# Placing K and Q on the diagonal by ScalarE, head by head, in a chunked delta-rule attention kernel

## The chip, the cores and the metric

The kernel runs on one core of a Trainium2 chip. The metric is the device time of one launch in microseconds (us). The kernel before was timed in three runs; a change of time is judged against their median.

## The reference

Three stages follow one another. Only the first, a gated delta rule over 4 batches, 8 heads, 768 positions and head size 48, is touched by the change:

```python
k_n = k / (norm(k) + 1e-6)
state = zeros((B, H, 48, 48))
for t in range(768):
    y[:, :, t] = q[t] @ state                     # per batch and head
    v_old = state.T @ k_n[t]
    state = state + beta[t] * outer(k_n[t], v[t] - v_old)
```

The second stage is a mixture of 8 experts with one expert per token (3072 tokens, 384 wide, 1024 hidden). The third is a gated feed-forward layer with 1536 hidden. All in float32.

## The kernel before, in words

The attention works in 24 steps of 32 positions. A step handles all 4 batches and 8 heads at once: two of the four batches share the 128 partitions (head dimension of one on rows 0 to 47, of the other on rows 64 to 111), and a second index p = 0, 1 tells the two such pairs apart. To multiply both batches of a pair in one matmul, the stationary operand is block diagonal: of its 64 columns, columns 0 to 31 hold the positions of the first batch and are zero on the lower rows, columns 32 to 63 hold those of the second and are zero on the upper rows. These operands are the tiles KB (12 of them, used in a ring, `RK`) and QB (two, in turn). Their layout is [128, p, 64 positions, 8 heads], so the 64 columns of one head lie 8 elements (32 bytes) apart.

A step s goes through these matmul groups on TensorE (PE), each of 16 products (8 heads, p = 0 and 1) unless noted; a float32 product shows as two instructions, so a group of 16 is listed as x32:

- KS: KB against the state SH; VectorE (DVE) then makes W from it (L802, L803).
- Y, first part: QB against the state (L818, and L859 for the six last products in steps from 19).
- U: TBD, the inverted triangle, against W (L827). ScalarE (ACT) and DVE split the result into UH, high and low.
- XTP: three transposes for the gate of the step before (`gate_t`).
- GP: KB of step s + 11 against KT, the raw K and Q of that step (`gp_mm`, L219), in two pieces, 24 instructions here and 8 later, for steps 1 to 12. The moving operand KT also has its columns 8 elements apart.
- Sps: the state's update in float16; ACT copies it to SH for the next step (L876).
- Y, second part, in float16, then GL, the gate's logits (12 instructions, stationary columns side by side).

DVE also computes, four steps at a time, the inverse of a 32 x 32 triangle for each of the 32 chunks (tiles X, Lt, XT). These many small operations are put between the others by a planner (`Filler`) with a fixed budget of modelled time for each step (`TA`, `TB`, `TP`); each engine executes its own instructions in the order written. The inverse of group 0 goes into TBD partly by copies, partly by a transfer on the queue of SyncE (SP) (`expand_rest`, L402).

Transfers of the attention are issued on SP's queue in the order written. In step s: KT of step s + 12 (`load_kt`), the diagonal of QB for step s + 1 (`fill`, two transfers), after KS the diagonal of KB for step s + 12 (`fill`, two transfers, for s up to 11), expansions of P and of normalized K (PBD, KBD), loads of K and V by token, and for s up to 4 `zero_fill` of one expert's first 512 rows in the dispatch table in HBM. `zero_fill` takes its zeros from half of TBD[1] and sends one row of 386 elements 16 times from each of 32 partitions. Before step 0, diagonals for steps 0 to 11 and three zero fills are issued in the same way. POOL (GpSimd) zeroes the off-diagonal blocks once, before the loop, and scatters finished rows to the dispatch table from step 6 on.

Of the kernel before, what the change touches and what calls it, by code (L numbers as in the profile page):

```python
# [7 lines left out]
F32 = mybir.dt.float32  # L8
# [13 lines left out]
NSTEP, NG = SEQ // CH, SEQ // CH // 4  # L22
# [3 lines left out]
STRIDE = 3136 + WIN  # L26
WINS = (460, 436, 416, 404, 396, 388, 380)
WMAX = 460
XMAX = 512
ROW = 386  # L30
# [4 lines left out]
LA = 11  # L35
# [35 lines left out]
RK = LA + 1  # L71
# [70 lines left out]
class Attention:  # L142
# [5 lines left out]
    def run(self, small, acc, zero_fill, small_loads):  # L148
        tc, a, beside = self.tc, self.a, self.beside
        nc = tc.nc  # L150
        V, A, G = [Queue(tc, e) for e in (nc.vector, nc.scalar, nc.gpsimd)]
        T, SP = Queue(tc, nc.tensor), Queue(tc, nc.sync)
        engines = (V, A, G, T, SP)
        ctx, early = ExitStack(), ExitStack()
        wk = ctx.enter_context(tc.tile_pool(name="at_w", bufs=1, side="right"))
# [13 lines left out]
        zf = cp.tile([128, 128], F16, name="zf")  # L169
        zl = cp.tile([128, 128], F16, name="zl")  # L170
        KB = [(ep if i < 8 else cp).tile([128, 2, 64, 8], F32, name=f"KB{i}") for i in range(RK)]
        QB = [cp.tile([128, 2, 64, 8], F32, name=f"QB{i}") for i in range(2)]
        TBD = [(cp if i else ep).tile([128, 32, 2, 32], F32, name=f"TBD{i}") for i in range(2)]
        PBD = [cp.tile([128, 2, 16, 4, 32], F16, name=f"PBD{i}") for i in range(2)]
        KBD = [cp.tile([128, 2, 2, 8, 2, 64], F16, name=f"KBD{i}") for i in range(2)]
# [9 lines left out]
        def fill(dst, s, k, rows=48):  # L185
            for par in range(2):
                r = slice(64 * par, 64 * par + rows)
                ins = SP.dma_start(
                    out=dst[r, :, 32 * par : 32 * par + 32].rearrange("p a t h -> p a (t h)"),
                    in_=a["st"][s, r].rearrange("p (k a x) -> p k a x", k=2, a=2)[:, k])  # L190
            return ins.ins

        def load_kth(u):
            t = wk.tile([128, 2, 48, 8], F32, tag="kth", name="kth", bufs=1)
            SP.dma_start(out=t.rearrange("p s d h -> p s (d h)"), in_=a["ktok"][:, 2 * u : 2 * u + 2])
            KTOK[u] = t

        def load_v(u):
            t = wk.tile([128, 2, 384], F32, tag="VT", name="VT", bufs=2)
            SP.dma_start(out=t, in_=a["vtok"][:, 2 * u : 2 * u + 2])  # L200
            VT[u] = t
# [10 lines left out]
        def gp_mm(s, hs, mm=T.matmul):  # L212
            if s not in GPS:
                tag = {4: "KS", 5: "Y", 7: "XTP", 8: "GL", 9: "U"}.get(s, "GP")
                GPS[s] = pool(tag).tile([128, 8, 64], F32, tag=tag, name="GP", bufs=1)
            ps, t = GPS[s], KT[s]
            for h in hs:
                for p in range(2):
                    mm(out=ps[64 * p : 64 * p + 64, h], lhsT=KB[s % RK][0:112, p, :, h], rhs=t[0:112, :, p, :, h], start=True, stop=True)  # L219

        G0 = {}

# [42 lines left out]
        def gp_evac(s):  # L265

            ps = GPS.pop(s)
            KT.pop(s)
            g, s4 = divmod(s, 4)
            if s4 == 0 and g > 0:  # L270
                GPM[g] = [ep.tile([128, 32, 32], F32, tag=n, name=n, bufs=b) for n, b in (("G", 2), ("P", 2))]
            A.copy(out=GPM[g][0][:, 8 * s4 : 8 * s4 + 8], in_=ps[:, :, 0:32])
            return A.copy(out=GPM[g][1][:, 8 * s4 : 8 * s4 + 8], in_=ps[:, :, 32:64]).ins
# [49 lines left out]
        def kexp(u):  # L323
            KH = KHG.pop(u)
            for b in range(4):
                SP.dma_start(
                    out=KBD[u % 2][32 * b : 32 * b + 32, :, :, :, b % 2, 0:48].rearrange("p s a h d -> p (s a h) d"),
                    in_=KH[32 * b : 32 * b + 32].rearrange("p s a h d -> p (s a h) d"))
# [56 lines left out]
                fil.step()  # L385

        XTS, others = {}, []
        zeros = TBD[1].rearrange("p k b i -> p (k b i)").rearrange("p (b x) -> p b x", b=2)

        def share_rows(n):  # L390
            for f in others[:n]:
# [231 lines left out]
        def zap_off(E, t):  # L623

            for par in range(2):
                r = t[64 * par : 64 * par + 64, :, 32 - 32 * par : 64 - 32 * par].rearrange("p a t h -> p a (t h)")
                E.memzero(r) if E is A else E.memset(r, 0.0)
# [46 lines left out]
        zap_off(G, KB[7])  # L674
        zap_off(A, KB[5])
        zap(A, PBD[0], 2)
        zap_off(G, QB[0])
        zap_off(G, QB[1])
        zap_off(G, KB[8])
        zap(G, PBD[1], 2)  # L680
        for i in range(9, RK):
# [74 lines left out]
        fil.run(99.0)  # L756
        load_kt(LA)
        fill(KB[LA], LA, 0, 64)
        fill(QB[1], 1, 1, 64)
        kexp(1)  # L760
        load_kth(2)
        zero_fill(SP, 2, zeros)
# [15 lines left out]
        for s in range(NSTEP):  # L778
# [8 lines left out]
            if s + 1 + LA < NSTEP:  # L787
                load_kt(s + 1 + LA)
            if 0 < s < NSTEP - 1:
                fill(QB[(s + 1) % 2], s + 1, 1, 64 if s == 1 else 48)  # L790
            beside(s, "load", engines)
            if s > 0:
                W = wk.tile([128, 8, 48], F32, tag="W", name="W", bufs=1)
# [4 lines left out]
            if s > 0:  # L798
                KSf = pp.tile([128, 512], F32, tag="KS", name="KS")
                KSp = KSf[:, 0:384].rearrange("p (h e) -> p h e", h=8)  # L800
                for h, p, r in hp:
                    mm(out=KSp[r, h], lhsT=KB[s % RK][:, p, :, h], rhs=S0[:, p, 48 * h : 48 * h + 48], start=True, stop=True)  # L802
                V.scalar_tensor_tensor(out=W, in0=vp, scalar=SIG * KSC, in1=KSp, op0=ALU.mult, op1=ALU.subtract)  # L803
            beside(s, "W", engines)
            if last:
                flush(gate_v1(g, 0, 2))
            if s + 1 + LA < NSTEP:
                fill(KB[s % RK], s + 1 + LA, 0)
            if s2 == 0 and 0 < s < NSTEP - 2:
                expand(PBD[(u + 1) % 2], PHL.pop(u + 1))  # L810
                if half:
# [3 lines left out]
            ny = NY if s >= LS else 16  # L815
            if s > 0:
                for h, p, r in hp[:ny]:
                    mm(out=Yp[r, h], lhsT=QB[s % 2][:, p, :, h], rhs=S0[:, p, 48 * h : 48 * h + 48], start=(h == 0), stop=False)  # L818
            beside(s, "Y", engines, Sps[0])

            Uf = pp.tile([128, 512], F32, tag="U", name="U", bufs=1)
# [11 lines left out]
            V.tensor_tensor(out=UH[:, 1], in0=Up, in1=UH[:, 0], op=ALU.subtract)  # L833
            if s4 == 0 and g in XE:
                expand_rest(g)
                fil.limit = g + 1
            if s2 == 0:
                if 0 < s < NSTEP - 2:
                    kh_split_lo(u + 1, V)
# [10 lines left out]
            if s == 0:  # L850
                gp_mm(LA, H8, mm)
                gp_evac(LA)
                zero2, other2, ops2 = inv_ops(2, SHE[2])
                fil.add(sum(prep(2), []) + [later(ops2)], 0.5)
            elif more:
                gp_mm(s + LA, H8[:GS], mm)
            else:
                for h, p, r in hp[ny:]:
                    mm(out=Yp[r, h], lhsT=QB[s % 2][:, p, :, h], rhs=S0[:, p, 48 * h : 48 * h + 48], start=(h == 0), stop=False)  # L859
            if last:  # L860
                gate_r(g, mm, 0, 2)
                ops = gate_v2(g, 0, 2)
# [46 lines left out]
            if more and s:  # L909
                gp_mm(s + LA, H8[GS:], mm)  # L910
                gp_evac(s + LA)
            if s == 0:
                expand(PBD[1], PHL.pop(1))
                kh_mul(2, 0)
                p_split(2)
                v_mul(2)
            elif half and s4 != 3:
                kh_mul(u + 2, s2)
                if s2:
                    kh_split_hi(u + 2)  # L920
            if s2 == 1 and half:
                load_v(u + 2)
            if s < 5:
                zero_fill(SP, s + 3, zeros)
            if s == 0:
                zero2()
            elif (s + LA) % 4 == 3 and (s + LA) // 4 < NG:
# [7 lines left out]
                kh_split_hi(u + 2)  # L935
            if s2 == 0 and 0 < s < NSTEP - 2:
                kexp(u + 1)
            beside(s, "end", engines)
            fil.run(((TB - (TP if s2 == 1 and u + 3 < NSTEP // 2 else 0.0) if s + 1 + LA < NSTEP else TC)) if s else TB0)
            if s4 == 3 and half and s < KL:  # L940
# [223 lines left out]
def kernel_body(tc, a, out):  # L1164
    nc = tc.nc
    V, A, G, T, SP = nc.vector, nc.scalar, nc.gpsimd, nc.tensor, nc.sync
    with ExitStack() as ctx:
# [10 lines left out]
        if True:  # L1178
# [6 lines left out]
                SP.dma_start(out=wgo, in_=a["wgo"])  # L1185

            def zero_fill(SP, e, z):
                r = XMAX // 32
                SP.dma_start(out=disp[e * STRIDE : e * STRIDE + 32 * r].rearrange("(p r) c -> p r c", r=r), in_=z[0:32, 1:2, 0:ROW].to_broadcast([32, r, ROW]))

            moe, late_pools = ExitStack(), ExitStack()
            gp = moe.enter_context(tc.tile_pool(name="gt_p", bufs=1, space=PSUM))
# [356 lines left out]
```

## Time and profile before

| what | value |
|---|---|
| median of 3 runs | 1077.36 us (1072.9 to 1080.02) |
| the profiled execution | 1079.89 us, span 1078.2 us |
| PE busy | 1021.3 us, 95% |
| DVE busy | 548.0 us, 51% |
| ACT busy | 397.2 us, 37% |
| POOL busy | 316.9 us, 29% |
| attention | about 0 to 349 us; step 1 begins at 69.05 |

The page of the profile shows for each engine its busy time as a share of the span, and the span in 40 slices. [...] In the slices the clock is at or near half for most of the attention and at full for nearly all that follows.

```profile
PE   9779999998889999899889999999999999999997
DVE  6968988989534577667683374511211211211111
ACT  7534544454453454445444422311212222212111
PEclk9875555665595999999999999999999999999999
DMA  7999988754584364556544122000000000000000
```

### The profile page before, as it was taken

What the parts mean: (1) busy time and instruction counts of PE and PEld (TensorE: products, weight loads), DVE (VectorE), ACT (ScalarE), POOL (GpSimd) and SP (SyncE); (2) the same over time, 40 slices, a digit from 0 to 9 for tenths busy, and PEclk for the clock granted to TensorE, in tenths of its full rate; (3) what the DMA queues carried; (4) which work ended last, traced back from release to release, by engine and by line L of the source; (5) the groups of instructions that cost most, each with busy time, mean ns of one, the idle gap of its engine ahead of it and who ended that gap; (6) DMA issues with size and microseconds to landing.
All of it is one profiled execution on the core that took longest, in us unless ns stands there. A gap on an engine that the chain in (4) does not pass through costs nothing. (4 is left out here: it accounts for less than half of the span.)

```text
span 1078.2 us, 22515 instructions
## 1 busy us (share of the span) xinstructions
PE 1021.3 (95%) x9111; PEld 923.9 (86%) x9112; DVE 548.0 (51%) x1498; ACT 397.2 (37%) x880; POOL 316.9 (29%) x304
## 2 busy tenths in 40 slices
PE   9779999998889999899889999999999999999997
PEld 8679888887889988789889988888888888888886
DVE  6968988989534577667683374511211211211111
ACT  7534544454453454445444422311212222212111
POOL 8530002202012234445444234322321311321322
PEclk9875555665595999999999999999999999999999
DMA  7999988754584364556544122000000000000000
GB/s 193 201 172 204 187 176 154 158 89 102 94 184 121 117 205 153 156 153 183 161 121 128 26 89 74 22 22 1 17 13 1 30 1 1 30 1 1 30 1 30
DMA packets 181438, 102.47 MB, mean 95 GB/s; under 512 B 126841, under 2 KB 170818, under 8 KB 181330
## 3 DMA queue, kind: packets, MB, share of 16 engines
q1 hardware_dynamic: 178258, 91.53, 36.8%
q0 software_dynamic: 3072, 9.46, 2.5%
q8 instruction: 73, 1.20, 0.5%
q14 instruction: 35, 0.29, 0.1%
HBM read 74.94 MB, written 15.80 MB: 84 GB/s over the span
## 5 line engine op out<-in xcount | busy, mean ns | idle before, releaser
L1470 DVE TENSOR_TENSOR gf<-gf,g 128x512 f32<-128x512 f32 x72 | 49.5, 687 | 310.1 <-PE g L1462 310.1
L971 POOL TENSOR_TENSOR gsl<-gf,gsh 128x512 fp32r<-128x512 f32 x68 | 88.4, 1300 | 272.4 <-ACT gsh L970 272.4
L1469 ACT ACTIVATE gf<-g 128x512 f32<-128x512 f32 x72 | 43.0, 597 | 188.5 <-PE g L1462 187.4
L970 ACT CAST gsh<-gf 128x512 fp32r<-128x512 f32 x69 | 42.8, 620 | 144.2 <-DVE gf L1470 142.5
L1436 PE MATMUL o<-woh,gsl 128*128 128x384 f32 x272 | 87.2, 339 | 0.0
L1436 PE MATMUL o<-wol,gsh 128*128 128x384 f32 x272 | 86.5, 337 | 0.0
L87 DVE TENSOR_TENSOR X<-X,tmp 128x84 f32<-128x84 f32 (+37 forms) x303 | 75.0, 277 | 0.8
L87 DVE TENSOR_TENSOR tmp<-X,Lt 128x84 f32<-128x84 f32 (+37 forms) x303 | 72.8, 271 | 1.4
L1151 DVE SCALAR_TENSOR_TENSOR hl<-h,hh 128x460 fp32r<-128x460 f32 (+7 forms) x57 | 33.0, 580 | 64.3 <-ACT hh L1150 64.2
L1110 PE MATMUL y<-hh,w2h 128*128 128x460 f32 (+6 forms) x168 | 60.9, 362 | 2.3 <-ACT hh L1150 2.1
L1462 PE MATMUL g<-yl,wgh 128*128 128x512 f32 x216 | 62.6, 395 | 0.0
L87 PE MATMUL U<-W,TBD 64*64 64x48 f32 x768 | 42.4, 283 | 21.2 <-DVE W L87 13.3
L1462 PE MATMUL g<-yl,wvh 128*128 128x512 f32 x216 | 62.3, 395 | 0.0
L1436 PE MATMUL o<-woh,gsh 128*128 128x384 f32 x272 | 61.7, 337 | 0.0
L87 POOL COPY XG<-g_sc 128x2 f32<-128x2 f32 x24 | 6.0, 248 | 187.5 <-DVE g_sc L87 145.4
L1462 PE MATMUL g<-yh,wgh 128*128 128x512 f32 x180 | 60.9, 395 | 0.0
L87 PEld LDWEIGHTS U<-W,TBD 64*64 64x64 f32 x768 | 38.6, 198 | 24.1 <-DVE W L87 14.9
L1110 PE MATMUL y<-hh,w2l 128*128 128x460 f32 (+6 forms) x168 | 58.6, 349 | 0.0
L87 ACT ACTIVATE ks<-kth,rnt 128x48 f32<-128x48 f32 x192 | 54.5, 371 | 6.9 <-DMA kth<-in_ktok_dram 6.8
L87 PE MATMUL GP<-KT,KB 112*64 112x64 f32 x640 | 47.9, 316 | 9.0 <-DMA KB<-in_st_dram 9.0
L1436 PEld LDWEIGHTS o<-woh,gsh 128*128 128x128 f32 x272 | 49.7, 188 | 5.8
L87 PEld LDWEIGHTS GP<-KT,KB 112*64 112x64 f32 x640 | 42.7, 221 | 13.7 <-POOL KH L87 8.3
(335 smaller groups left out, 2420.1 us busy)
## 6 DMA issues: line engine op xcount, KB each, us to landing
w1r<-in_w_dram SPq DMA_DIRECT2D x32, 384.0 KB
w2r<-in_w_dram SPq DMA_DIRECT2D x32, 384.0 KB
KT<-in_st_dram SPq DMA_DIRECT2D x20, 448.0 KB
disp<-TBD SPq DMA_DIRECT2D x8, 772.0 KB
kth<-in_ktok_dram SPq DMA_DIRECT2D x12, 384.0 KB
VT<-in_vtok_dram SPq DMA_DIRECT2D x12, 384.0 KB
KBD<-KH SPq DMA_DIRECT2D x48, 96.0 KB
XG<-in_m2g_dram SPq DMA_DIRECT2D x12, 384.0 KB
```

The costliest lines, as they stand in the source:

```text
L87: r = f(*args, **kw)
L970: (act or nc.scalar).copy(out=hi, in_=src)
L971: eng.tensor_tensor(out=lo, in0=src, in1=hi, op=ALU.subtract)
L1110: self.T.matmul(out=ys[c][:, 0:n], lhsT=w2[l][:, f % 2, 128 * c : 128 * c + 128], rhs=(hh, hl)[r], start=(f == 0 and i == 0), stop=(f == 7 ...
L1151: self.V.scalar_tensor_tensor(out=hl, in0=hp[:, 0:n], scalar=0.0, in1=hh, op0=ALU.max, op1=ALU.subtract)
L1436: T.matmul(out=ops_[m][:, 0:384], lhsT=gh[l][:, 128 * m : 128 * m + 128], rhs=wo[r][:, f], start=(f == 0 and i == 0), stop=(f == 11 and i ...
L1462: T.matmul(out=ps, lhsT=gv[w][l][:, c, 128 * f : 128 * f + 128], rhs=Y[r][c], start=(i == 0 and c == 0), stop=(i == 2 and c == 2))
L1469: A.activation(out=gf, in_=gps[0], func=AF.Sigmoid)
L1470: V.tensor_tensor(out=gf, in0=gf, in1=gps[1], op=ALU.mult)
```

## The change

QB and the KB tiles that are used a second time (steps 12 to 23) get the layout [128, p, 8 heads, 64 positions], so the columns of one head lie side by side (`kcol`, `by_col`). They are no longer filled by transfers. Two copies on ACT (`place`) take rows 0 to 63 and rows 64 to 111 of raw data that lie in SBUF and write them into the diagonal blocks. For K the raw data is KT, which is loaded anyway; for Q it is a new tile QR with one buffer, loaded by one transfer of 112 rows (`load_q`). `place` for Q of step s + 1 and K of step s + 12 stands at the end of step s, behind the copies of GP from PSUM. POOL zeroes a whole KB tile in each of the steps 0 to 11, since the new layout has its zeros elsewhere. K of steps 0 to 11 keeps the old layout and its transfers. `zero_fill` sends four rows in one run of 1544 elements from each of 128 partitions; its zeros now lie in parts of TBD[1] that group 1's inverse needs first, so experts 3 to 7 are zeroed in steps 0 to 2 in place of steps 0 to 4, and the planner may finish group 1 only from the end of step 2 on (`fil.limit`).

```diff
-        QB = [cp.tile([128, 2, 64, 8], F32, name=f"QB{i}") for i in range(2)]
+        QB = [cp.tile([128, 2, 8, 64], F32, name=f"QB{i}") for i in range(2)]
...
+        by_col = lambda t: t.rearrange("q p t h -> q (p t h)").rearrange("q (p h t) -> q p h t", p=2, h=8)
+        def kcol(s, p, h):
+            return KB[s % RK][:, p, :, h] if s < RK else by_col(KB[s % RK])[:, p, h]
+        def place(dst, src):
+            for par, n in ((0, 64), (1, 48)):
+                r = slice(64 * par, 64 * par + n)
+                A.copy(out=dst[r, :, :, 32 * par : 32 * par + 32], in_=src[r].rearrange("q p t h -> q p h t"))
+        def load_q(s):
+            t = wk.tile([128, 2, 32, 8], F32, tag="QR", name="QR", bufs=1)
+            SP.dma_start(out=t[0:112].rearrange("q p t h -> q (p t h)"), in_=a["st"][s, 0:112, 512:1024])
+            QR[s] = t
...
-                    mm(out=ps[64 * p : 64 * p + 64, h], lhsT=KB[s % RK][0:112, p, :, h], rhs=t[0:112, :, p, :, h], start=True, stop=True)
+                    mm(out=ps[64 * p : 64 * p + 64, h], lhsT=kcol(s, p, h)[0:112], rhs=t[0:112, :, p, :, h], start=True, stop=True)
...
-        fill(QB[1], 1, 1, 64)
+        load_q(1)
...
             if 0 < s < NSTEP - 1:
-                fill(QB[(s + 1) % 2], s + 1, 1, 64 if s == 1 else 48)
+                load_q(s + 1)
...
-                    mm(out=KSp[r, h], lhsT=KB[s % RK][:, p, :, h], rhs=S0[:, p, 48 * h : 48 * h + 48], start=True, stop=True)
+                    mm(out=KSp[r, h], lhsT=kcol(s, p, h), rhs=S0[:, p, 48 * h : 48 * h + 48], start=True, stop=True)
...
             if s + 1 + LA < NSTEP:
-                fill(KB[s % RK], s + 1 + LA, 0)
+                zap(G, KB[s % RK])
...
-                    mm(out=Yp[r, h], lhsT=QB[s % 2][:, p, :, h], rhs=S0[:, p, 48 * h : 48 * h + 48], start=(h == 0), stop=False)
+                    mm(out=Yp[r, h], lhsT=QB[s % 2][:, p, h], rhs=S0[:, p, 48 * h : 48 * h + 48], start=(h == 0), stop=False)
...
-                fil.limit = g + 1
+                fil.limit = g + 1 if g else 0
...
             if more and s:
                 gp_mm(s + LA, H8[GS:], mm)
                 gp_evac(s + LA)
+            if s + 1 < NSTEP:
+                place(QB[(s + 1) % 2], QR.pop(s + 1))
+            if s + 1 + LA < NSTEP:
+                place(by_col(KB[s % RK]), KT[s + 1 + LA][:, 0])
...
-            if s < 5:
-                zero_fill(SP, s + 3, zeros)
+            if s < 3:
+                for e in ((3, 4), (5, 6), (7,))[s]:
+                    zero_fill(SP, e, zeros)
...
+            if s == 2:
+                fil.limit = 1
...
             def zero_fill(SP, e, z):
-                r = XMAX // 32
-                SP.dma_start(out=disp[e * STRIDE : e * STRIDE + 32 * r].rearrange("(p r) c -> p r c", r=r), in_=z[0:32, 1:2, 0:ROW].to_broadcast([32, r, ROW]))
+                SP.dma_start(out=disp[e * STRIDE : e * STRIDE + XMAX].rearrange("(p r) c -> p (r c)", r=XMAX // 128), in_=z[:, 0 : XMAX // 128 * ROW])
```

## Rows read from the trace of the kernel before

**Rows 1.** Busy time by stretch of late steps: stretch, PE, PEld, DVE, ACT, POOL, clock, DMA.

```profile
296.00:322.00 26.00, 22.92 (x534) 21.52 (x531) 9.40 (x25) 13.52 (x35) 3.28 (x5) 1.00 0.85 185
322.00:350.00 28.00, 28.00 (x471) 25.52 (x469) 12.41 (x48) 9.05 (x22) 5.71 (x10) 0.51 0.49 122
```

**Rows 2.** The same view of step 2 and step 3, each from KS to KS.

```profile
87.23:100.59 13.36, 12.60 (x220) 11.77 (x219) 13.26 (x49) 6.15 (x17) 0.00 (x0) 0.50 1.07 208
100.59:113.10 12.51, 12.51 (x220) 11.75 (x219) 10.91 (x39) 6.63 (x18) 0.00 (x0) 0.50 0.91 190
```

**Rows 3.** What PE waited for, 20 to 345 us: total us, times, longest us.

```profile
PE U L87 <- DVE W L87: 13.3, 9, 3.8
PE GP L87 <- DMA KB<-in_st_dram: 9.0, 2, 8.2
PE U L87 <- DMA TBD<-XT: 7.8, 4, 3.8
```

**Rows 4.** Timeline of PE in step 7, clock 0.5: start, duration, instructions, count.

```profile
154.20 2.10 PE L87 MATMUL KS<-SH,KB 128*64 128x48 f32 x32
156.09 2.14 PE L87 MATMUL Y<-SH,QB 128*64 128x48 f32 x32
...
165.53 0.83 PE L87 MATMUL GL<-wgo,xt 128*64 128x16 f32 x12
166.19 0.72 PE L87 MATMUL GP<-KT,KB 112*64 112x64 f32 x8
```

**Rows 5.** Timeline of PE at clock 1.0, steps 12 and 19.

```profile
224.59 1.76 PE L87 MATMUL GP<-KT,KB 112*64 112x64 f32 x24
...
299.63 2.11 PE L87 MATMUL KS<-SH,KB 128*64 128x48 f32 x32
301.56 1.38 PE L87 MATMUL Y<-SH,QB 128*64 128x48 f32 x20
302.87 1.13 PE L87 MATMUL U<-W,TBD 64*64 64x48 f32 x32
303.94 0.55 PE L87 MATMUL XTP<-cst,XG 128*128 128x128 f32 x3
```

**Rows 6.** Timeline of SP's queue before and in step 0, transfers of KB.

```profile
49.48 1.32 SPq L87 DMA_DIRECT2D KB<-in_st_dram  x2
...
67.79 3.35 SPq L87 DMA_DIRECT2D KB<-in_st_dram  x2
```

**Rows 7.** Timeline of PE around the two longest waits for transfers.

```profile
55.41 2.25 PE L87 MATMUL GP<-KT,KB 112*64 112x64 f32 x32 [8.15 <-DMA KB<-in_st_dram]
...
78.71 1.91 PE L87 MATMUL U<-W,TBD 64*64 64x48 f32 x30 [1.36 <-DMA TBD<-XT]
```

**Rows 8.** DMA rate in 40 slices of 30.0 to 34.3, a zero fill alone.

```profile
GB/s 205 158 244 206 186 201 230 244 244 249 263 172 259 230 244 230 215 201 215 187 244 230 215 201 129 215 201 201 215 187 187 172 201 215 187 230 172 115 206 29
```

**Rows 9.** The same of 68.4 to 72.0, a load's end and a zero fill.

```profile
GB/s 325 427 394 377 326 463 360 412 343 377 360 309 309 309 292 223 206 274 223 206 223 240 189 189 223 245 137 223 223 137 206 223 120 223 189 148 302 643 188 410
```

**Rows 10.** Timeline of ACT in step 7.

```profile
154.71 0.38 ACT L87 COPY P<-GP 128x256 f32<-128x256 f32 x1
155.11 2.29 ACT L87 ACTIVATE ks<-kth,rnt 128x48 f32<-128x48 f32 x8
160.16 0.48 ACT L87 CAST UH<-U 128x384 f16<-128x384 f32 x1 [2.76 <-PE U L87]
```

**Rows 11.** Instructions by tile, ACT and POOL: count, shortest/median/longest ns, first and last start.

```profile
L87 ACT CAST PHL<-P x10: 601/610/622, 81.0 to 291.3; 128x512 f16<-128x512 f32 x10
L87 ACT CAST KH<-ks x24: 494/504/512, 31.0 to 310.1; 128x384 f16<-128x384 f32 x24
L87 ACT ACTIVATE ks<-kth,rnt x192: 361/370/395, 26.6 to 309.5; 128x48 f32<-128x48 f32 x192
L1040 ACT ACTIVATE XR<-XR x24: 600/602/620, 391.5 to 570.1; 109x384 f32<-109x384 f32 x4, 104x384 f32<-104x384 f32 x4, 101x384 f32<-101x384 f32 x4, 99x384 f32<-99x384 f32 x4
L87 POOL MEMSET QB<- x4: 518/520/523, 9.9 to 11.6; 64x512 f32 x4
```

More of the change, by code (lines that the diff above doesn't have):

```diff
@@ L196, in load_kth @@
             KTOK[u] = t
+        by_col = lambda t: t.rearrange("q p t h -> q (p t h)").rearrange("q (p h t) -> q p h t", p=2, h=8)
[5 more added lines that the diff above has]
+                A.copy(out=dst[r, :, :, 32 * par : 32 * par + 32], in_=src[r].rearrange("q p t h -> q p h t"))
+        QR = {}
+        def load_q(s):
+            t = wk.tile([128, 2, 32, 8], F32, tag="QR", name="QR", bufs=1)
+            SP.dma_start(out=t[0:112].rearrange("q p t h -> q (p t h)"), in_=a["st"][s, 0:112, 512:1024])
+            QR[s] = t
         def load_v(u):
@@ L387, in run @@
         XTS, others = {}, []
-        zeros = TBD[1].rearrange("p k b i -> p (k b i)").rearrange("p (b x) -> p b x", b=2)
+        zeros = TBD[1].rearrange("p k b i -> p (k b i)")
         def share_rows(n):
@@ L676, in run @@
         zap(A, PBD[0], 2)
-        zap_off(G, QB[0])
-        zap_off(G, QB[1])
+        zap(G, QB[0])
+        zap(G, QB[1])
         zap_off(G, KB[8])
@@ L858, in run @@
                 for h, p, r in hp[ny:]:
-                    mm(out=Yp[r, h], lhsT=QB[s % 2][:, p, :, h], rhs=S0[:, p, 48 * h : 48 * h + 48], start=(h == 0), stop=False)
+                    mm(out=Yp[r, h], lhsT=QB[s % 2][:, p, h], rhs=S0[:, p, 48 * h : 48 * h + 48], start=(h == 0), stop=False)
             if last:
```

## The prediction

> **What bounds the kernel now.** I read the slices first: TensorE (PE) is busy nearly everywhere, and from 349 us on it runs the experts and the last layer, which the change leaves alone. So everything happens in the first 349 us. There I cut the time at each KS group, one step a row. Two kinds of step alternate [rows 2]. In step 2 DVE is busy 13.26 of 13.36 us and PE waits for it; in step 3 PE is busy 12.51 of 12.51 us and DVE has 1.6 us to spare. Both run at clock 0.50. PE's waits come next [rows 3]: nine times U waits for W, 13.3 us in all, which is DVE at its limit; 9.0 us go to loads of KB ahead of the loop, 7.8 us to transfers into TBD. Late in the attention DVE is nearly free (9.40 of 26 us) and PE is the bound, at clock 1.00 from 296 to 322 us and 0.51 after that [rows 1]. POOL is idle in both steps of rows 2, ACT half busy.
>
> **The transfers before step 2.** The two longest waits outside DVE lie here [rows 7]: GP waits 8.15 us for the KB of step 10, and in step 1 the U group is held, last by 1.36 us, by the triangle's transfer (rows 3 has its longest piece, 3.8). A zero fill alone moves about 210 GB/s [rows 8]: 512 rows of 1544 bytes, 0.79 MB, take 3.8 us. Where longer runs of a load are mixed in, the rate is 310 to 460 [rows 9]; at 400 a fill takes 2.0 us. One row of 1544 bytes per run becomes four, from four times the partitions. The fill of expert 1 stands ahead of the KB that GP waits for: up to 1.8 us earlier, and the loop with it. In step 0 the fill of expert 2 (1.8 us) and the two KB transfers, which hold SP's queue 3.35 us [rows 6] and are gone, stand ahead of the triangle's transfer. Its wait of 3.8 + 1.36 = 5.2 us shrinks by 3.2 (1.8 for the fill, 1.0 for 192 KB at 200 GB/s, 0.4 for Q of step 1, now smaller). Sum 1.8 + 3.2 = 5.0 us gained. If short runs are not what makes a fill slow, 1.4 remain; if the wait goes wholly, 1.8 + 5.2 = 7.0.
>
> **Stationary columns side by side.** At half clock KS takes 1.89 us from its start to Y's, 16 pairs of 118 ns; GL, whose stationary columns already touch, takes 0.66 us for 6 pairs, 110 ns [rows 4]. So at half clock 16 pairs gain 0.13 us. At full clock KS takes 1.93 us, no less than at half, while U, with touching columns, takes 1.07 [rows 5]: 0.86 us for 16 pairs. GP keeps a moving operand 32 bytes apart and its 12 pairs take 1.76 us at full clock [rows 5]; whether stationary or moving columns hold it no row shows, so between 0 and 0.13 us for 16 pairs at half clock, 0 to 0.86 at full. I take half, as both operands look alike.
>
> [...]
>
> Steps 2 to 12: only the five steps bound by PE (3, 5, 7, 9, 11) can pay it out, 0.13 for Y and 0.07 for GP each: 1.0 us. The others wait for W anyway. Steps 13 to 23: KS and Y both gain. In the half-clock steps 15, 17, 22 and 23 that is 0.26 each, 1.0 us. Steps 18 and 19 run at full clock and could gain 1.7 each, but W (DVE) no longer hides behind Y, and ACT has copies to do before UH; I take 0.75 each, 1.5 us. Step 20's gain goes into the triangle's transfer of group 5, one of the four waits of rows 3. That is 2.5 us for steps 13 to 23, with 2 to 12 3.5; 1 to 6.
>
> **The price on ACT.** Each step issues two copies of 512 elements for Q, and up to step 11 two for K. No copy of this shape is in the trace. Low end: PHL, 512 touching elements, 0.61 us [rows 11]. High end: ks reads 48 elements 32 bytes apart with a scale from memory, 0.370 us. Touching, it should take KH's 0.504 less 336 elements at 0.83 ns (PHL less KH, 0.106 us over 128), 0.225, and 0.1 for the scale (XR 0.602 against KH 0.504): 0.325. The 0.045 left are 0.94 ns an element, so 512 cost 0.48 more: 1.09 us. ks reads with the same step on the same engine; but its excess may be fixed, so I take 0.85.
>
> [...]
>
> Where it lies: in step 7 the copy of P ends at 155.09 and Y starts at 156.09 [rows 4, 10]. Two copies (back to back 0.1 less for the second) take 1.1 to 2.1 us, so Y waits 0.1 to 1.1, at my value 0.6. In the DVE-bound steps that hides in the wait for W; five PE-bound steps pay it, 3.0 us (0.5 to 5.5). Then K's copies and ks stand ahead of UH, where ACT idles 2.76 us [rows 10]: four copies of 2.2 to 4.2 us make UH up to 1.4 late. PE has 24 GP instructions (1.76 us) behind U to cover UH's 0.48 and DVE's share; DVE, where full, waits. I take 0.5 us in two steps, 1.0 (0 to 4). From step 13 on GP is gone and the copies sit behind x_evac with more room: nothing.
>
> Cheap items: zeroing KB costs POOL 12 x 1.0 us (twice 0.52, rows 11) where it idles [rows 2]; it has until the step's end. Whether a memset slows DVE beside it no row shows: 0 taken, since POOL works while ends are set elsewhere; at worst the memset's 1.0 us in six DVE-bound steps, 6 us. The late limit for group 1 costs nothing as long as DVE is still at that inverse at the end of step 2, which rows 2 make likely.
>
> **Clock.** It is 0.50 in steps 2 and 3 although PE is busy 12.51 of 12.51 us in one [rows 2], 1.00 from 296 to 322 us and 0.51 from there on [rows 1]: full clock comes and goes in stretches that look alike. Denser matmuls may bring it up earlier or hold it. At full clock KS, Y and U of a late step would take 1.07 us each [rows 5] in place of about 1.8, 2.2 us, and the groups behind them a little less too: 2.5 us a step. Of the four half-clock steps 15, 17, 22 and 23 I take two: 5.0 (0 to 10).
>
> **Sum.** -5.0 (transfers) - 1.0 (steps 2 to 12) - 2.5 (13 to 23) + 3.0 + 1.0 (ACT) - 5.0 (clock) = -9.5 us. The profiled execution is 1079.89 us, its span 1078.2 with 1.7 around it, 2.5 above the median. The difference goes on the median, 1077.4 - 9.5: **1068 us**, its own range 1062 to 1075. One per cent, about what a measurement here can tell from no change, is 10.8 us: 1066.6 or 1088.2.
>
> **Rivals.**
> - *The clock stays up* (0.25). For: KS gains nothing from full clock today, so a warm stretch is half wasted. Against: every second early step keeps its wait for W. The other two late steps save 2.5 each, the five PE-bound early ones about 0.8: 1068 - 9, 1059; faster.
> - *The copies hold ACT's queue* (0.13; the side that loses). `place` waits in order for KT and QR, and behind it stand ks, UH and SH. A load issued at 49.48 let GP start only at 55.41 [rows 6, 7], some 6 us later, with the DMA engines full; with shares of 0.91 to 1.07 in steps 2 and 3 [rows 2] that is likely until the zero fills are done, and for K the use moves forward from the next step's GP to this step's end. It decides once a load lands more than 1 us after the copies of GP. At 3 us in each of steps 1 to 6 (18) and the copies at the high end (5.5 more): 1068 + 23.5, about 1091; slower. Against: two KB transfers and part of each fill leave the queue, and KT is issued early in most steps.
> - *The copies eat the gain* (0.14): high end in all steps, 9.5 instead of 4, and no clock: 1068 + 5.5 + 5 = about 1079; same.
> - *The change doesn't speed loading* (0.05): other limits hold KS at 118 ns; the transfers' gain less ACT's price: about 1076; same.
>
> **How the numbers follow.** The forecast has 0.43. About 0.35 of it lies under 1066.6, 0.15, the rest, 0.28, within 1%. Faster: 0.15 + 0.25 = 0.40. Same: 0.28 + 0.14 + 0.05 = 0.47, with 0.01 of the third rival's tail 0.46. Slower: 0.13 and that 0.01, 0.14. The range goes from 1053 (clock up, all bounds good) to 1084 (copies dear, POOL beside DVE) and leaves out the queue rival and a little below.
>
> **What would show it.** Step 1's KS earlier by about 2 us, U of step 1 waiting under 3 us; zero fills of 2 us. Y's 16 pairs 1.76 us at half clock and near 1.0 at full. Copies into QB between 0.61 and 1.09 us, Y late by 0.6 in odd steps. ACT waiting for a transfer in front of a copy speaks for the queue; a clock row above 0.60 between 84 and 280 us for the clock. I am wrong if step 2 starts no earlier, or if the odd steps come out longer than 13 us.

## The result, and the profile after

The changed kernel takes 1090.98 us (median of nine runs, 1089.57 to 1092.98) against 1079.74 of the kernel before beside it: ratio 1.0115, 95% interval 1.0089 to 1.0141 (the ratio is estimated from all the runs; the two medians alone give 1.0104). It is slower by 1.2%; 1068 was forecast, and 1084 was the upper end. The profiled execution took 1091.71 us, its span 1090.0.

The page of the profile first: in the attention, the first 13 slices, ACT has become a busy engine and PE shows gaps. The clock (PEclk, TensorE's granted clock in tenths of full speed) is higher than before in the early slices and at half where it used to rise.

```profile
PE   9787988878898999999899999999999999999997
DVE  6968998979523667767774375511311311311111
ACT  6557878876665454445354432312212212221121
PEclk8877667665555799999899999999999999999999
```

Next, what PE waited for up to 365 us (total us, times, longest), which answers to [rows 3]. A wait that did not exist heads the list: 21 times Y stands behind a copy into QB. U's waits for W are no shorter than before; the transfers ahead of the loop gained 3.0 us and the triangle's 2.4.

```profile
PE Y L87 <- ACT QB L87: 21.8, 21, 3.9
PE U L87 <- DVE W L87: 14.2, 9, 3.4
PE GP L87 <- DMA KB<-in_st_dram: 6.0, 2, 4.9
PE U L87 <- DMA TBD<-XT: 5.4, 3, 2.8
PE Sps L87 <- ACT UH L87: 4.3, 4, 1.8
```

ACT's groups of 60 to 365 us show the price of a copy beside the row that was taken for its low end (busy us, mean ns of one):

```profile
L87 ACT COPY QB<-QR 64x512 f32<-64x512 f32 (+1 forms) x46 | 52.0, 1130 | 2.5 <-DMA QR<-in_st_dram 2.2
L87 ACT COPY KB<-KT 64x512 f32<-64x512 f32 (+1 forms) x24 | 27.3, 1137 | 3.2 <-DMA KT<-in_st_dram 2.8
L87 ACT CAST PHL<-P 128x512 f16<-128x512 f32 x10 | 6.1, 609 | 0.0
```

In the timelines of PE and of ACT in step 7 (start, duration, instructions; the wait in brackets) one follows it. ACT gets to Q's copies when P is out of PSUM, 153.39, and is done 2.27 us later; KS is long over, and Y begins at 155.71, 1.15 late. K's copies and ks then keep ACT busy until UH starts, at 160.19, without a pause; [rows 10] had 2.76 us to spare in front of it.

```profile
152.50 2.06 PE L87 MATMUL KS<-SH,KB 128*64 128x48 f32 x32
155.71 1.95 PE L87 MATMUL Y<-SH,QB 128*64 128x48 f32 x32 [1.15 <-ACT QB L87]
157.59 1.89 PE L87 MATMUL U<-W,TBD 64*64 64x48 f32 x32
159.41 0.55 PE L87 MATMUL XTP<-cst,XG 128*128 128x128 f32 x3
159.89 1.61 PE L87 MATMUL GP<-KT,KB 112*64 112x64 f32 x24
```

```profile
153.00 0.38 ACT L87 COPY P<-GP 128x256 f32<-128x256 f32 x1
153.39 2.27 ACT L87 COPY QB<-QR 64x512 f32<-64x512 f32 x2
155.68 2.29 ACT L87 COPY KB<-KT 64x512 f32<-64x512 f32 x2
158.00 2.28 ACT L87 ACTIVATE ks<-kth,rnt 128x48 f32<-128x48 f32 x8
160.19 0.45 ACT L87 CAST UH<-U 128x384 f16<-128x384 f32 x1
```

SP's queue, 60 to 365 us, has a new wait at its head too: 15 times it is held until ACT has emptied QR, which has one buffer. In the kernel before SP waited for ACT 1.5 us at most.

```profile
SPq L87 <- ACT QB L87: 59.4, 15, 9.9
SPq L87 <- PE GP L87: 30.9, 5, 8.2
```

Last, the attention in two long stretches, KS of step 2 to KS of step 14 and on to KS of step 21 (stretch, busy time of PE, PEld, DVE, ACT, POOL, clock, DMA). First before, then after:

```profile
87.23:241.95 154.72, 145.52 (x2568) 136.22 (x2566) 140.79 (x562) 77.29 (x215) 16.55 (x16) 0.57 0.84 159
241.95:315.67 73.72, 65.88 (x1291) 61.66 (x1289) 48.23 (x191) 37.36 (x106) 10.51 (x16) 0.64 0.61 127
```

```profile
83.84:244.69 160.85, 131.11 (x2568) 120.38 (x2564) 142.28 (x564) 128.05 (x262) 21.60 (x26) 0.70 0.65 140
244.69:327.43 82.74, 71.49 (x1290) 65.47 (x1289) 48.21 (x191) 53.71 (x121) 9.99 (x16) 0.50 0.56 118
```

Step 2 starts 3.4 us earlier. Up to step 14 PE works 14 us less, at a higher clock, and the stretch is 6.1 us longer: PE idles 29.7 us in place of 9.2. In the second stretch PE works 5.6 us more and idles 3.4 more: 9.0 us, the clock at 0.50 throughout. The rest of the attention loses 2.4 and the experts win 2.3 back. Summed, with the 3.4 us of lead taken off, that makes 11.8 us, the difference of the two spans.

### The profile page after: what moved, and what is told of

It reads as the page before. It is cut to its first block, busy times and chain, and to the rows that moved or that the text cites. A ratio compares the mean times of both kernels' runs of the same rounds, so it can differ in the third digit from the quotient of the medians.

```text
span 1090.0 us, 22564 instructions
## 1 busy us (share of the span) xinstructions
PE 1012.6 (93%) x9111; PEld 910.9 (84%) x9112; DVE 548.6 (50%) x1498; ACT 474.6 (44%) x950; POOL 323.3 (30%) x314
## 5 line engine op out<-in xcount | busy, mean ns | idle before, releaser
L87 PE MATMUL U<-W,TBD 64*64 64x48 f32 x768 | 45.0, 293 | 21.9 <-DVE W L87 14.2
L87 PEld LDWEIGHTS U<-W,TBD 64*64 64x64 f32 x768 | 41.1, 208 | 24.9 <-DVE W L87 15.5
L87 PE MATMUL Y<-SH,QB 128*64 128x48 f32 x736 | 40.0, 282 | 21.9 <-ACT QB L87 21.8
L87 PEld LDWEIGHTS Y<-SH,QB 128*64 128x64 f32 x736 | 35.8, 196 | 26.5 <-ACT QB L87 25.1
L87 ACT COPY QB<-QR 64x512 f32<-64x512 f32 (+1 forms) x46 | 52.0, 1130 | 2.5 <-DMA QR<-in_st_dram 2.2
```

The source lines that it names most:

```text
L87: r = f(*args, **kw)
```

## The experiments

Ratios are to the kernel before, run on the same chip beside each kernel, with 95% intervals. The lengths come from one profiled execution of each kernel, cut at KS as above.

| kernel | median us | ratio | steps 2 to 13 (clock) | steps 14 to 20 (clock) |
|---|---|---|---|---|
| before | | 1 | 154.7 (0.57) | 73.7 (0.64) |
| changed | 1090.98 | 1.0115 (1.0089 to 1.0141) | 160.9 (0.70) | 82.7 (0.50) |
| a1 | 1076.39 | 0.9984 (0.9969 to 0.9999) | 156.6 (0.52) | 78.3 (0.53) |
| a3 | 1086.27 | 1.0091 (1.0065 to 1.0118) | 155.2 (0.77) | 77.9 (0.61) |
| a4 | 1096.67 | 1.0173 (1.0142 to 1.0205) | 165.4 (0.50) | 79.2 (0.52) |
| c1 | 1073.36 | 0.9927 (0.9902 to 0.9953) | 152.3 (0.81) | 78.7 (0.55) |
| c2 | 1083.72 | 1.0015 (0.9989 to 1.0042) | 159.0 (0.73) | 81.1 (0.50) |
| c3 | 1080.18 | 1.0003 (0.9978 to 1.0027) | 156.4 (0.53) | 70.8 (0.72) |
| c4 | 1074.61 | 0.9938 (0.9902 to 0.9973) | 151.1 (0.66) | 77.9 (0.53) |
| d1 | 1074.03 | 0.9913 (0.9870 to 0.9955) | 156.5 (0.52) | 70.9 (0.74) |
| d2 | 1073.21 | 0.9918 (0.9894 to 0.9942) | 149.8 (0.65) | 74.2 (0.66) |
| e1 | 1075.21 | 0.9948 (0.9924 to 0.9973) | 152.3 (0.80) | 78.5 (0.54) |
| e2 | 1069.11 | 0.9884 (0.9864 to 0.9904) | 150.4 (0.72) | 68.5 (0.72) |
| f1 | 1081.22 | 0.9996 (0.9960 to 1.0032) | 156.7 (0.54) | 82.2 (0.50) |
| f2 | 1074.43 | 0.9978 (0.9942 to 1.0014) | 164.5 (0.52) | 76.2 (0.55) |
| f3 | 1072.50 | 0.9947 (0.9914 to 0.9980) | 158.7 (0.74) | 76.9 (0.55) |

### Parts of the change by themselves

**a1**, on the kernel before, only the zero fills and their limit:

```diff
-            if s < 5:
-                zero_fill(SP, s + 3, zeros)
+            if s < 3:
+                for e in ((3, 4), (5, 6), (7,))[s]:
+                    zero_fill(SP, e, zeros)
...
```

> The kernel before with only the transfers of the change that concern the zero fills: four rows a run, two fills at the end of steps 0 and 1, one at the end of step 2, and the limit on the planner's work for group 1. K and Q still come by transfers. Theory A (the transfers are a gain and the loss is in ACT's copies of Q): the fills take about 2 us instead of 3.8, GP ahead of the loop waits 4.9 us instead of 8.15, step 2's KS starts 2 to 4 us before 87.23, no wait of Y, steps 18 to 21 at about 8.2 us as before; 1073 to 1077 us on the scale where before is 1079.7, ratio 0.994 to 0.998. Rival C (the fills moved together, two at a time, cost later transfers their place): steps 3 to 6 longer than before, the lead of step 2 gone by step 6, ratio 1.000 or more. Rival B (the late clock is lost for reasons outside the copies, such as the shifted phase of the steps): steps 18 to 21 near 10.8 us at clock 0.50 here too, ratio 1.005 to 1.01.

Step 2's KS starts at 83.80, as early as in the changed kernel, so all of that lead is the fills'. A fill alone goes at about 400 GB/s now (the changed kernel, 18 slices between 247 and 525) in place of the 210 of [rows 8]. Whether the longer runs or the four times as many partitions make it faster was not separated. Little of it reaches the end: 0.16%, at the edge of what was expected, with steps 17 to 19 at clock 0.50 in the profiled execution. Steps 3 to 6 cost 0.3 us more than before, so the fills pushed nothing aside; theory C falls.

**a2**, on the changed kernel, Q placed for the first steps only:

```diff
-            if s + 1 < NSTEP:
+            if s < 2:
                 place(QB[(s + 1) % 2], QR.pop(s + 1))
```

> The changed kernel without ACT's copies of Q from step 3 on: the placing of Q is left out, Y multiplies an old Q; the loads of Q and all copies of K stay. Theory A: the 21.8 us in which Y waits for a copy fall to under 2, ACT is busy some 45 us less, and since steps 14 to 23 no longer stall before Y the clock comes back to 0.8 to 1.0 in steps 18 to 21 (8 us a step): 1070 us or less against 1091 of the changed kernel. Rival B (the late clock does not hang on these stalls): Y's waits go, 8 to 12 us come back, but steps 18 to 21 stay at 0.50 and above 10 us: 1079 to 1083. Rival C (transfers of the first steps): steps 0 to 2 as in the changed kernel, no gain from the copies beyond 3 us, since U then waits for W instead: 1087 or more.

The stages behind the attention, whose work follows Y's values, take far longer with an old Q, and the total of 1352 us can't be compared, which the expectation overlooked. The attention can: steps 2 to 13 take 152.9 us and 14 to 20 76.9, 13.9 us less than in the changed kernel. But the clock in steps 14 to 20 is 0.56 and, after 0.67 in step 15, rises only in step 20 (0.85): the copies' absence doesn't by itself bring it.

**a4**, K as before, Q on ACT:

```diff
...
-                zap(G, KB[s % RK])
+                fill(KB[s % RK], s + 1 + LA, 0)
...
-            if s + 1 + LA < NSTEP:
-                place(by_col(KB[s % RK]), KT[s + 1 + LA][:, 0])
```

> The changed kernel with K as before: by transfers onto the diagonal, positions 8 elements apart, no zeroing of KB in the loop and no copies of K; Q still by copies. Theory A (Q's copies are the loss, K's side is small): Y's waits stay at 19 to 22 us, KS takes 1.89 us at half clock and 1.9 at full; steps 1 to 12 within 2 us of the changed kernel in sum, 1088 to 1094. Rival (K's copies, 24 of 1.14 us ahead of ks and UH, carry a good part of the loss): UH's waits on DVE fall from 20 to about 12 and steps 2 to 12 get shorter by 4 us or more: 1082 to 1087.

0.6% slower than the changed kernel, where both theories had about the same or faster. K on ACT is a gain. Without it the clock is 0.50 in each of steps 2 to 13, and Y's waits stay: 17.5 us, U's for the triangle 12.0.

**c1**, the other half, K on ACT and Q by transfers as before:

```diff
...
-                load_q(s + 1)
+                fill(QB[(s + 1) % 2], s + 1, 1, 64 if s == 1 else 48)
...
-            if s + 1 < NSTEP:
-                place(QB[(s + 1) % 2], QR.pop(s + 1))
```

> The changed kernel with Q as before: two transfers a step onto QB's diagonal, positions 8 elements apart, no copies of Q; K stays with ACT, head by head, and the zero fills four to a run. By the runs so far the change has three parts: transfers of the first steps -1.4 us (a1 against before), Q on ACT +20.3 (a4 1096.67 less a1 1076.39), K on ACT -5.7 (the changed kernel 1090.98 less a4 1096.67). If the parts add (theory): no wait of Y for a copy, granted clock of 0.6 to 0.9 in steps 2 to 12 as in every run with K head by head, 1070.7 us; 1068 to 1074. Rival (K's copies only looked cheap because Q's copies held the step anyway): UH late, DVE waits, 1077 to 1082.

It beats both kernels, by 0.7% and 1.9%. The parts add: a1 to c1, K on ACT, is -0.57%, and from a4 to the changed kernel it is -0.58%; Q on ACT costs 1.9% by either pair. The whole loss is Q's.

### What Q's copies cost with

**a3**, the copies of Q behind the copy of the gate's transposes:

```diff
             if s > 0:
                 gate_t(s - 1)
+                if s + 1 < NSTEP:
+                    place(QB[(s + 1) % 2], QR.pop(s + 1))
...
-            if s + 1 < NSTEP:
+            if s == 0:
                 place(QB[(s + 1) % 2], QR.pop(s + 1))
```

> The changed kernel with the two copies of Q for the next step moved within ACT's order: from the end of the step to right behind the copy of the gate's transposes, where ACT idled about 2.3 us at half clock before it copies the state. All work is done. Theory A: Y's waits (21.8 us) fall to under 4 us; up to 1 us a step moves to the state's copy SH at full clock, where that gap is only 0.9 us; 1076 to 1084 us, and lower if steps 18 to 21 come back to clock 1.0. Rival B: Y's waits go but steps 18 to 21 keep 0.50: 1081 to 1086. Rival (ACT as a whole is the bound, not the place of the copies): KS or Sps then waits for ACT as long as Y did, 1089 to 1093.

By its ratio the rival is nearest: Y's waits are gone but for 0.7 us, and in their place KS waits for the state and U for W. Only KS's 9.3 us are a wait for ACT, though. U's 30.2 us for W (DVE) stand in a2 as well, which has no copies of Q there, so that wait needs no late copy. The profiled execution, 1080.54 us, is the fastest of the four by 5 us, so the whole loss isn't in this trace.

```profile
PE U L87 <- DVE W L87: 30.2, 12, 4.2
PE KS L87 <- ACT SH L87: 9.3, 7, 4.5
```

**c2**, a second buffer for QR:

```diff
-            t = wk.tile([128, 2, 32, 8], F32, tag="QR", name="QR", bufs=1)
+            t = wk.tile([128, 2, 32, 8], F32, tag="QR", name="QR", bufs=2)
```

> The changed kernel with a second buffer for QR, the raw Q that ACT copies from; nothing else. In the changed kernel SP's queue waits 59.4 us in 15 pieces for ACT to be done with QR, and the triangle's transfers and the prefetches of the experts behind it start late. Theory (the price is the copies' own time in front of Y, 21.8 us of waits): SP's waits go, Y's waits stay at 18 to 22 us, U's waits for the triangle fall from 5.4 to about 3: 1087 to 1090. Rival (the held queue is the price): 1080 or less, with Y's waits falling too, since the copies themselves were late.

Neither had the time; of the waits, the theory was right. One digit in the code takes back 1.0% of the 1.15%, although Y waits as long as ever; what shrinks is U's wait for the triangle (PE's waits up to 365 us):

```profile
PE Y L87 <- ACT QB L87: 22.3, 21, 3.5
...
PE U L87 <- DMA TBD<-XT: 1.6, 1, 1.6
```

So the held queue is a price of its own beside the copies, with the clock at 0.50 in steps 14 to 20 of both kernels. Step 21 shows it: in the changed kernel SP stands at QR until 319.31, then issues four transfers for the experts, P's expansion, 8.14 us long, and the triangle's pieces at 329.97, 2.5 us after that step's KS. U waits 4.05 us for them in two pieces (2.58 in the kernel before).

```profile
319.31 0.32 SPq L87 DMA_DIRECT2D QR<-in_st_dram  x1
319.68 0.42 SPq L87 DMA_DIRECT2D w1r<-in_w_dram  x1
...
321.78 8.14 SPq L87 DMA_DIRECT2D PBD<-PHL  x4
329.97 2.76 SPq L87 DMA_DIRECT2D TBD<-XT  x4
```

In c2 the pieces go out at 317.65, 4.9 us ahead of that step's KS, and U doesn't wait. Of the 6.3 us that the attention gains from step 2 on in these two executions, 2.8 lie behind step 20 and the rest in small pieces before it.

**e1** and **e2**, on c1, a dummy that holds the queue, with one buffer and with two:

```diff
...
+            t = wk.tile([128, 8], F32, tag="QR", name="QR", bufs=1)   # e2: bufs=2
+            SP.dma_start(out=t[0:112], in_=a["st"][s, 0:112, 512:520])
...
+            if s + 1 < NSTEP:
+                A.copy(out=wk.tile([128, 8], F32, tag="QS", name="QS", bufs=1)[0:112], in_=QR.pop(s + 1)[0:112])
```

> The kernel with K alone on ACT (c1, ratio 0.9927) and one dummy: at the place of the load of raw Q a transfer of 8 elements a row into a tile with one buffer, which ACT reads in one small copy at the place of Q's copies. Q itself comes by transfers as before. So SP's queue is held as in the changed kernel, until ACT is at the step's end, while the copies cost nothing. Theory (the held queue is a price by itself): SP waits for ACT some 40 to 60 us, U waits longer for the triangle, ratio 1.000 to 1.004, 8 to 12 us above c1. Rival (the hold hurts only when the copies in front of Y are long, or through the larger load): 0.992 to 0.996.

> The same dummy with two buffers, the control: the same transfers and copies, but SP is not held. Both theories: 0.992 to 0.995, as c1. If it comes out as high as the dummy with one buffer, it is the additional transfer or the small copy that costs, and not the hold.

Against its control e1 is 0.64% slower, the intervals apart, some 7 us: less than was expected, and e1 alone lies where the rival put it, 0.2% from c1 and inside the intervals. SP is held less as well, 21.7 us in 8 pieces against 59.4 in 15:

```profile
SPq L87 <- ACT QS L87: 21.7, 8, 6.9
```

e2 came out at 0.9884, the fastest of all, though it is c1 with a dummy added. Their intervals touch; c1's profiled execution is at clock 0.55 in steps 14 to 20, e2's at 0.72, so the difference is likely the clock's and not the dummy's. The same holds between e1 and e2: their profiles differ by 10.0 us in steps 14 to 20, at 0.54 and 0.72, and it is in e2, which isn't held, that U waits longer for the triangle (7.4 us against 2.4). So this pair doesn't show the hold as a price. That rests on c2, and on d1 below.

**c3**, an input array with the positions of a head side by side, for KT and QR:

```diff
...
-                A.copy(out=dst[r, :, :, 32 * par : 32 * par + 32], in_=src[r].rearrange("q p t h -> q p h t"))
+                A.copy(out=dst[r, :, :, 32 * par : 32 * par + 32], in_=src[r])
...
+        "sth": c(st.reshape(nc_, 128, 4, CH, NH).swapaxes(3, 4)).reshape(nc_, 128, 1024),
```

> The changed kernel with one more input array that holds the raw K and Q of a step with the 32 positions of a head side by side (a layout made on the host, as the present one is); KT and QR are loaded from it, so ACT's copies read touching elements, and GP's moving operand touches too. Placement, buffers and order are unchanged. Theory (a copy costs 1.12 us because its source lies 32 bytes apart): copies of 0.55 to 0.65 us; Y's waits fall from 21.8 us to 2 to 6 (the two copies of Q then take as long as PE needs for KS and less), and some 10 us come back: 1076 to 1082. If the 1.12 us come from the target or from the size, copies stay above 1.0 and the time at 1089 to 1092.

As expected. The copies take half the time (ACT's groups, 60 to 365 us), so the stride was the price; Y's waits fall to 4.0 us.

```profile
L87 ACT COPY QB<-QR 64x512 f32<-64x512 f32 (+1 forms) x46 | 28.3, 615 | 1.5 <-DMA QR<-in_sth_dram 1.2
```

**d1**, c2 and c3 together, and **d2**, with a3's order as well (their edits are those shown):

> The changed kernel with both mends: the additional input array, so that ACT's copies read touching elements (c3), and a second buffer for QR (c2). Each alone took the ratio to the kernel before from 1.0115 to 1.000 (c3) and 1.0015 (c2). Theory (two prices, the copies' length in front of Y and SP's queue held by the one buffer, that add): 1.0115 - 0.011 - 0.010, about 0.990, 1067 to 1073 on the scale where before is 1079; Y's waits under 5 us, U's waits for the triangle under 5. Rival (one price seen from two sides: a shorter copy lets go of the queue earlier, and so each mend alone has taken it all): 0.998 to 1.001.

> As the kernel with both mends, and Q's copies moved to right behind ACT's copy of the gate's transposes. Theory: what is left of Y's waits (2 to 5 us) goes, and since a copy is 0.6 us now, the two fit into ACT's gap ahead of the state's copy: 1 to 3 us less, ratio 0.987 to 0.990, a candidate to beat the others. Rival (as in a3 the state's copy SH is late then, KS waits): within 1 us of the kernel with both mends or above it.

d1: two prices that add, 1.1% and 1.0%; 0.991 as expected. Its profiled execution, the slowest of its six, is as long as c3's in both stretches of the table, and step 21 differs as in c2: there U waits 7.0 us for the triangle in c3, where SP stood 40.9 us at QR in all, and 2.5 in d1, where it doesn't stand there. d2 gains nothing on it, since KS waits 6.0 us for the state: the place is worth nothing once a copy is short. **c4**, c1 with the additional array for KT:

```diff
...
-                    mm(out=ps[64 * p : 64 * p + 64, h], lhsT=kcol(s, p, h)[0:112], rhs=t[0:112, :, p, :, h], start=True, stop=True)
+                    mm(out=ps[64 * p : 64 * p + 64, h], lhsT=kcol(s, p, h)[0:112], rhs=t[0:112, :, p, h], start=True, stop=True)
```

> The kernel with Q by transfers and K on ACT, and the additional array for KT alone: K's copies and GP's moving operand read touching elements. A candidate to beat both kernels. Theory (what is left of K's price is its copies, 24 of 1.14 us, ahead of ks and UH): copies of 0.6 us, GP's 24 instructions at full clock shorter than 1.57 us, 1 to 4 us less than the kernel with K alone on ACT, 1066 to 1071. Rival (UH is not late, ACT has room): within 1 us of it.

0.1% from c1, well inside the intervals: the rival, K's copies had room in ACT. GP's touching operand, which c3 and d1 have as well, gains nothing measurable here, so c3's 1.1% is not put down to it.

### The late steps' clock

On d1, **f1** and **f2** issue Q's copies twice, in the late or the early steps; **f3** is c2 with the touching source from step 13 on:

```diff
-                place(QB[(s + 1) % 2], QR.pop(s + 1))
+                for _ in range(2 if s >= 12 else 1):   # f2: s < 12
+                    place(QB[(s + 1) % 2], QR[s + 1])
```

```diff
...
+            SP.dma_start(out=t[0:112], in_=a["sth" if s > 12 else "st"][s, 0:112, 512:1024])
...
```

> The kernel with both mends (touching source, two buffers, ratio 0.9913), in which from the end of step 12 on each of the two copies of Q is issued twice, to the same place: ACT's time in front of Y is again some 2.3 us a step, in the late steps alone. Theory (the late clock hangs on the stall): steps 17 to 19 fall from 0.77 to 1.00 to 0.50 and from 8 to 10.5 us, 8 to 12 us more, ratio 0.999 to 1.003. Rival (only the length counts): the clock stays at 0.77 to 1.00 in steps 17 to 19, some 0.5 to 1 us of wait in each of eleven steps, 4 to 8 us, ratio 0.995 to 0.998.

> The same with the copies doubled up to the end of step 11 and single from then on. Both theories: Y waits 0.5 to 1.5 us in steps 3 to 12, of which the steps that wait for W anyway hide a part: 4 to 8 us more than with both mends, ratio 0.995 to 0.998; steps 17 to 19 stay at 0.77 to 1.00. If the ratio stays at 0.991 the early stalls cost nothing and the loss is all late.

> The changed kernel with two buffers for QR (c2, ratio 1.0015), in which Q from step 13 on is loaded from the additional array, so that its copies read touching elements; up to step 12 they stay at 1.13 us. Theory: Y's waits of steps 14 to 23 go, steps 17 to 19 come up from 0.50 and 10.8 us to 0.77 to 1.00 and 8 us: 8 to 12 us less, ratio 0.990 to 0.994. Rival: only the waits themselves (some 4 us) come back, steps 17 to 19 stay at 0.50: ratio 0.996 to 0.999.

f1 falls as the theory has it, from 0.9913 to 0.9996, some 9 us. Steps 14 to 20 of d1, then of f1:

```profile
241.44:312.30 70.86, 55.93 (x1291) 51.63 (x1289) 48.10 (x191) 45.83 (x121) 10.30 (x16) 0.74 0.65 135
```

```profile
239.94:322.10 82.16, 71.50 (x1290) 65.40 (x1289) 48.06 (x191) 54.95 (x135) 10.32 (x16) 0.50 0.61 125
```

PE's idle time is lower in f1 (10.7 us against 14.9) and its busy time 15.6 higher: in this pair the loss is the clock, not the wait. f2 costs more in steps 2 to 13, 8.0 us by the profile; but its steps 17 to 19 are at 0.50, which both theories excluded, and its clock rises in step 20 (0.55 in the mean of steps 14 to 20). f3 comes out between theory and rival, with steps 17 to 19 at 0.50 too and the clock up in step 20 (0.55 in the mean as well).

Over all traces: with copies of over 2 us a step in front of Y in the late steps (changed, c2, a4, f1) no step from 14 to 19 is above 0.50, and of the four only a4 comes up in step 20 (0.76). The thirteen without them all come to 0.68 or more in one of the steps 17 to 20, six of them by step 18. That and f1 speak for the stall putting the full clock off. But the other seven, f2 and f3 among them, come up only in step 20, no earlier than a4 with its copies; f1's ten runs lie between 1073.56 and 1087.98, and each kernel was profiled once: what fixes the step stays open, and so does how the 22 us divide between waits and clock.

## Why the prediction was wrong

**The step that failed** is the price on ACT, +4.0 us. It measured 1.0115 less d1's 0.9913, 2.0% or 22 us. Three things were off.
- *The copy*: 0.85 us was taken, 1.13 measured, just past the high end of 1.09. "but its excess may be fixed, so I take 0.85" was the wrong choice: c3 shows 0.615 without the stride, so each of 512 elements costs 1.0 ns more, as the 0.94 worked out from ks says, and that row should have tipped it.
- *Who pays*: "five PE-bound steps pay it" and "from step 13 on ... nothing". Y waited 21 times in 23 steps, 1.0 us in the mean, and eight of these (3.7 us) lie after step 13. That the wait hides in the wait for W where DVE is the bound was right in part: U waits 14.2 us for W, but 22.1 in c1, which has the same K and no copies of Q. By this pair some 8 of Y's 21.8 us are hidden and some 14 are left, where 3.0 were forecast; a2, without the copies, is 13.9 us shorter in steps 2 to 20. Behind the late stalls stands the clock, in f1 at least (0.50 in steps 14 to 20 against d1's 0.74).
- *A queue not looked at*: the load of Q was booked as a gain, because two transfers became one. That it stands in SP's order and must wait for QR's one buffer until ACT is at the end of the step was not priced; c2 makes that 1.0%. This term stood at nothing in the sum.

**The rival at 1091** had the time by luck, since it had not the place. It put 18 of its 23.5 us into ACT waiting for transfers. ACT waited 2.8 and 2.2 us, once each; it was SP that waited for ACT. Its other part, copies at the high end, holds, and was too low at 5.5.

**Transfers before step 2, -5.0.** Step 2's KS came 3.4 us earlier, fills go at the rate taken (about 400 GB/s), and GP's wait fell from 8.15 to 4.9. At the end 1.7 us (0.16%) are left of it in a1. The worst case of the cheap items, POOL's zeroing slowing DVE, did not come: DVE is busy 141.1 us in steps 2 to 13 of c1, which zeroes KB, and 140.9 in a1, which doesn't.

**Columns, -3.5, and clock, -5.0.** At full clock KS now takes 1.11 us for its 32 instructions (step 13) and 1.93 at half (step 21), against 2.11 and 2.10 in [rows 4, 5]: both sizes about as forecast. For GP "half" was wrong. At clock 1.00 its 24 instructions take 1.76 us with both operands apart [rows 5], 1.61 with the stationary columns alone side by side (step 7 above), and 0.92 with the moving ones as well (c4, step 5, where XTP takes the 0.55 of [rows 5]): the moving columns hold it. Even so K on ACT brought 0.57%, 6 us, with steps 2 to 13 at 0.81 in c1 against 0.52 in a1. The rival "the clock stays up" had that right for the early steps, but not for the late ones: c1, without Q's stalls, is at 0.55 in steps 14 to 20. There the clock term, two steps taken as an estimate without a row that shows what raises the clock, came out the other way. None of the steps 15, 17, 22 and 23 rose in the changed kernel, and steps 18 to 20, at 0.76 to 1.00 before, ran at 0.50 and took 31.5 us in place of 24.2.

So the sum comes out about right where ACT's price is small: d1, where Y waits 5.0 us in all and SP doesn't stand at QR, is at -0.87%, 9.4 us, and -9.5 was forecast with +4.0 for ACT. That the totals meet is partly luck: the transfers gave 1.7 of 5.0, K on ACT more than its columns were priced at, and d1 has GP's touching operand, which the change does not have (c4 gained nothing by it).

## What to carry to other kernels

Here a load into a tile with one buffer tied its queue to the reader (SP stood 59.4 us at QR, and c2's second buffer took back 1.0%): look where the last read of the old contents stands in the reader's order, and what is queued behind the load. A copy put in front of a matmul in every step is to be priced at the high bound when its read has a stride that a row of the same engine already shows as dear (0.94 ns an element from ks, 1.0 measured), and only as much of its wait is hidden as a longer wait behind it takes in (some 8 of Y's 21.8 us). Change both operands of a matmul to touching columns before counting on the full clock's rate: GP's 24 instructions took 1.61 us at clock 1.00 with one changed and 0.92 with both.

## What the runs showed of the hardware

ACT's float32 copy of 512 elements takes 0.615 us when its source touches and 1.13 us when the elements lie 32 bytes apart (c3 and the changed kernel). The granted clock in steps 2 to 13 went with the layout of K in a way not foreseen: 0.50 to 0.57 with both of GP's operands apart (before, a1, a4), 0.70 to 0.81 with K's columns side by side and the moving ones apart (changed, a2, a3, c1, c2, e1, e2, f3), and 0.52 to 0.66 with both side by side (c3, c4, d1, d2, f1, f2). Why is not shown.
